# Output projection, feed-forward output and final step on two column tiles, two stores, and row sums ahead of a group's last PV

## The chip, the cores and the metric

The kernel runs on one core of a Trainium2 chip. The metric is the device time of one execution in microseconds (us): 202.74, the median of three runs from 202.69 to 202.88.

## The reference

Eight sequences have one new token each. A decode step of attention over the last 1024 positions of a key and value cache and a small feed-forward block both start from the same row of 448 numbers, and a sigmoid gate mixes their results. Cut to what matters:

```python
x = A_x                                               # 8 x 1 x 448
g = sigmoid((x * gate_w).sum(-1, keepdims=True))
q = x @ wq                                            # 16 heads of 256
k, v = k_cache[:, :, -1024:], v_cache[:, :, -1024:]   # 8 kv heads, each for 2 query heads
p = softmax((q . k) * 256 ** -0.5)
a = concat_heads(p . v) @ wo                          # 4096 -> 448
h = gelu(layernorm(x) @ w1 + b1)                      # 448 -> 1792
b = h @ w2 + b2                                       # 1792 -> 448
return g * a + (1 - g) * b                            # 8 x 1 x 448
```

## The kernel before

All inputs and the output are bf16; sums are kept in float32 in PSUM. A *pair* is one sequence with one kv head: 64 pairs, numbered so that eight in a row share a kv head and make a *group* of eight pairs. Each pair has a K tile and a V tile of 512 KB, and each group has 448 KB of `wo` (`wo_sb[g]`). The kernel reads 78 MB in all.

**Order of the loads.** Lines 121 to 135 issue the small inputs, `w1`, `w2` and `wq` on SP's and ACT's queues. Lines 137 to 164 then lay out one list for SP's queue: K tiles, V tiles eleven pairs behind them, the `wo` part of a group behind its last K tile, and at the very end the last V tiles and `wo_sb[7]`. The K and V tiles share 23 buffers; `issue_to` (line 148) issues the first 23 at once and then one for each tile that has been used.

**Front.** `transposed` (207), `mlp_up` (231) and `mlp_down` (258) do the feed-forward block. `mlp_down` adds 14 matmuls and one for the bias into `b_ps` (lines 261 and 268): the stationary operand is `hT`, with 8 columns for the 8 sequences, and 448 columns of `w2` stream past it. Line 272 scales the result by 1 - g into `bvec`. Lines 280 to 299 make the queries.

**Main loop** (432 to 455), written out by hand, each engine working in program order. Step n transposes the K tile of pair n on TensorE (line 314) and copies it from PSUM on VectorE (319), computes the scores of pair n-1 (330), and does the PV product of pair m = n-11 (396). Once for each group come the maximum (`soft_max1`, `soft_max2`), the exponential (`soft_exp`), and, behind the PV of its last pair, `soft_sum` (380: eight matmuls that add up the rows of the exponentials, line 382, and a reciprocal, 387), `o_scale` (405: the scaling of the PV results into `ot`, line 407). One step later `o_proj` (415) multiplies the group's `ot` by its part of `wo`: four matmuls (421), 8 columns stationary, 448 streamed, all added into `A_ps`. Scores, row sums and PV results of a group lie in one PSUM tile, `grp`.

**End.** Behind the loop stand the last `o_proj` (456), the final step on VectorE, res = A_ps * g + bvec (458), and one store on SP's queue (461).

Of the kernel before, what the change touches and what calls it, by code (L numbers as in the profile page):

```python
# [9 lines left out]
ALU = mybir.AluOpType  # L10
AXIS = mybir.AxisListType
BF16 = mybir.dt.bfloat16
F32 = mybir.dt.float32
# [3 lines left out]
def kernel(  # L17
# [15 lines left out]
    nc = tc.nc  # L33
    P = nc.NUM_PARTITIONS

    B, Sq, D = A_x.shape
    _, Hkv, Sk, Dh = A_k_cache.shape
    HD = A_wq.shape[1]
    Hq = HD // Dh
    rep = Hq // Hkv  # L40
# [3 lines left out]
    NB = B  # L44
    NJ = Dh // P
    NC = W // P
    NF = F // P
# [10 lines left out]
    NKV = 23  # L58


    S0 = 0
    O0 = S0 + NC * R
    Z0 = O0 + NJ * R
# [3 lines left out]
    out_f = out.rearrange("b s d -> (b s) d")  # L67

    consts = ctx.enter_context(tc.tile_pool(name="consts", bufs=1))
# [9 lines left out]
    ps_a = ctx.enter_context(  # L79
        tc.tile_pool(name="ps_a", bufs=1, space=bass.MemoryType.PSUM)  # L80
    )
# [10 lines left out]
    w2_sb = consts.tile([P, NF, D], BF16, name="w2_sb")  # L92
    b2_sb = consts.tile([1, D], BF16, name="b2_sb")
    NKH = rep * NJ
    wo_sb = [consts.tile([P, NKH, D], BF16, name=f"wo_sb{g}") for g in range(Hkv)]
    ident = consts.tile([P, P], BF16, name="ident")
    identf = consts.tile([P, P], F32, name="identf")
    onesb = consts.tile([P, P], BF16, name="onesb")
# [2 lines left out]
    xT = consts.tile([P, DC + 2, NB], BF16, name="xT")  # L101
    yT = consts.tile([P, DC + 1, NB], BF16, name="yT")
    x_e = consts.tile([NB, 2, P], BF16, name="x_e")
    g_sb = consts.tile([NB, 1], F32, name="g_sb")
    omg_sb = consts.tile([NB, 1], F32, name="omg_sb")
    bvec = consts.tile([NB, D], F32, name="bvec")
    res = consts.tile([NB, D], BF16, name="res")


    def k_src(src, n):  # L110
# [58 lines left out]
    for t in diag:  # L169
        nc.gpsimd.memset(t[:], 0.0)  # L170
    nc.gpsimd.memset(x_e[:], 0.0)
    nc.gpsimd.tensor_copy(identf[:], ident[:])
    nc.vector.memset(yT[:], 1.0)


# [2 lines left out]
    gth = consts.tile([NB, 1], F32, name="gth")  # L178
# [15 lines left out]
        y_sb[:], x_sb[:], scalar1=mv[:, 0:1], scalar2=rstd[:],  # L194
        op0=ALU.subtract, op1=ALU.mult,
    )
    nc.vector.tensor_scalar(g_sb[:], gth[:], 0.5, 0.5, op0=ALU.mult, op1=ALU.add)
    nc.vector.tensor_scalar(omg_sb[:], g_sb[:], -1.0, 1.0, op0=ALU.mult, op1=ALU.add)

    A_ps = ps_a.tile([NB, D], F32, name="A_ps")  # L200

    for h in range(2):
        nc.vector.tensor_copy(
# [25 lines left out]
    M = {}  # L229
# [27 lines left out]

    def mlp_down():
        b_ps = ps_g.tile([P, 512], F32, tag="grp", name="b_ps")
        for k in range(NF):  # L260
            nc.tensor.matmul(  # L261
                b_ps[0:NB, 0:D],
                lhsT=M["hT"][:, k * NB : (k + 1) * NB],
                rhs=w2_sb[:, k, :],
                start=(k == 0),
                stop=False,
            )
        nc.tensor.matmul(  # L268
            b_ps[0:NB, 0:D], lhsT=onesb[0:1, 0:NB], rhs=b2_sb[:],
            start=False, stop=True,  # L270
        )
        nc.vector.tensor_scalar_mul(bvec[:], b_ps[0:NB, 0:D], omg_sb[:])  # L272

    mlp_up()
    mlp_down()


    q_ps = ps_g.tile([P, 512], F32, tag="grp", name="q_ps")
    NQ = Hq * NJ
    for c in range(DC + 1):  # L280
        for k in range(NQ):
            if c < DC:
                w, xs = wq_sb[:, c, k * P : (k + 1) * P], xT[:, c, :]
            else:
                h, kk = divmod(k, NQ // 2)
                w, xs = wq_t[:, kk * P : (kk + 1) * P], xT[:, DC + h, :]
            nc.tensor.matmul(
                q_ps[:, k * NB : (k + 1) * NB],
                lhsT=w,
                rhs=xs,  # L290
                start=(c == 0 and k == 0),
                stop=(c == DC),
                skip_group_check=True,
# [14 lines left out]
    def transposes(n):  # L308
        K = KV.pop(("K", n))
        kt = ktpool.tile([P, NJ, W], BF16, tag="kt", name="kt")  # L310
        for j in range(NJ):
            ktp = ps_kt.tile([P, W], BF16, tag="ktp", name="ktp")
            for c in range(NC):
                nc.tensor.transpose(  # L314
                    ktp[:, c * P : (c + 1) * P],
                    K[:, c, j * P : (j + 1) * P],
                    ident[:],
                )
            nc.vector.tensor_copy(kt[:, j, :], ktp[:])  # L319
        KT[n] = kt  # L320

    def scores(n):
        g, b = divmod(n, NB)
        kt = KT.pop(n)
        if b == 0:
            G[g] = ps_g.tile([P, 512], F32, tag="grp", name="grp")
        for c in range(NC):
            for j in range(NJ):
                s = S0 + c * R + b * rep
                nc.tensor.matmul(  # L330
                    G[g][:, s : s + rep],
                    lhsT=kt[:, j, c * P : (c + 1) * P],
                    rhs=qT[:, j, g, b, :],
                    start=(b == 0 and c == 0 and j == 0),
                    stop=(j == NJ - 1),
                    skip_group_check=True,
                )

    def soft_max1(g):
        pm = work.tile([P, R], F32, tag="pm", name="pm")  # L340
        nc.vector.reduce_max(
            pm[:],
            G[g][:, S0 : S0 + NC * R].rearrange("p (c r) -> p r c", r=R),
            axis=AXIS.X,
        )
        G["pm", g] = pm
# [22 lines left out]
    def soft_exp(g):  # L369
        nc.tensor.matmul(  # L370
            G[g][:, S0 : S0 + NC * R].rearrange("p (c r) -> p c r", c=NC),
            lhsT=onesb[:],
            rhs=diag[g % 2][:].unsqueeze(1).to_broadcast([P, NC, R]),
            start=False, stop=True, skip_group_check=True,
        )
        e = work.tile([P, NC * R], BF16, tag="e", name="e")
        nc.scalar.activation(e[:], G[g][:, S0 : S0 + NC * R], ACT.Exp)  # L377
        E[g] = e

    def soft_sum(g):  # L380
        for c in range(NC):
            nc.tensor.matmul(  # L382
                G[g][:, Z0 : Z0 + R], lhsT=onesb[:], rhs=E[g][:, c * R : (c + 1) * R],
                start=False, stop=(c == NC - 1), skip_group_check=True,
            )
        rz = work.tile([P, R], F32, tag="rz", name="rz")
        nc.vector.reciprocal(rz[:], G[g][:, Z0 : Z0 + R])  # L387
        RZ[g] = rz

    def pv(m):  # L390
        g, b = divmod(m, NB)
        V = KV.pop(("V", m))
        for j in range(NJ):
            for c in range(NC):
                o = O0 + j * R + b * rep
                nc.tensor.matmul(  # L396
                    G[g][:, o : o + rep],
                    lhsT=V[:, c, j * P : (j + 1) * P],
                    rhs=E[g][:, c * R + b * rep : c * R + (b + 1) * rep],
                    start=False,  # L400
                    stop=(c == NC - 1),
                    skip_group_check=True,
                )

    def o_scale(g):
        ot = work.tile([P, NJ, R], BF16, tag="ot", name="ot")
        nc.vector.tensor_tensor(  # L407
            ot[:],
            G[g][:, O0 : O0 + NJ * R].rearrange("p (j r) -> p j r", j=NJ),
            RZ[g][:].unsqueeze(1).to_broadcast([P, NJ, R]),  # L410
            op=ALU.mult,
        )
        OT[g] = ot

    def o_proj(g):
        ot = OT[g]
        for i in range(rep):
            for j in range(NJ):
                k = i * NJ + j
                w = wo_sb[g][:, k, :]  # L420
                nc.tensor.matmul(  # L421
                    A_ps[:],
                    lhsT=ot[:].rearrange("p j (b i) -> p j i b", i=rep)[:, j, i, :],
                    rhs=w,
                    start=(g == 0 and k == 0),
                    stop=(g == Hkv - 1 and k == NKH - 1),
                )


    LAST = NPAIR + NB + LAG  # L430
# [1 line left out]
    for n in range(LAST):  # L432
        if n < NPAIR:
            transposes(n)
            done += 1
        if 0 <= n - 1 < NPAIR:
            scores(n - 1)
        g, r = divmod(n, NB)
        if g >= 1 and g - 1 < Hkv:
            if r == 0:  # L440
                soft_max1(g - 1)
            if r == 1:
                soft_max2(g - 1)
            if r == 2:
                soft_exp(g - 1)
        m = n - NB - LAG
        if m >= 0:
            pv(m)
            done += 1
            if m % NB == NB - 1:  # L450
                soft_sum(m // NB)
                o_scale(m // NB)
            if m % NB == 0 and m > 0:
                o_proj(m // NB - 1)
        issue_to(NKV + done)
    o_proj(Hkv - 1)

    nc.vector.scalar_tensor_tensor(  # L458
        res[:], in0=A_ps[:], scalar=g_sb[:], in1=bvec[:], op0=ALU.mult, op1=ALU.add
    )  # L460
    nc.sync.dma_start(out_f, res[:])


# [1 line left out]
_INS = ['A_x', 'A_k_cache', 'A_v_cache', 'A_wq', 'A_wo', 'B_x', 'B_w1', 'B_b1', 'B_w2', 'B_b2', 'gate_w']  # L465
_OUTS = [((8, 1, 448), 'bfloat16')]
# [25 lines left out]
```

## Time and profile before

| | us |
|---|---|
| median of three runs | 202.74 |
| the profiled execution | 202.94 |
| its span, first to last instruction | 201.2 |
| PE (matmul) busy | 161.7 |
| PEld (weight load) busy | 146.6 |
| DVE (VectorE) busy | 106.7 |
| ACT (ScalarE) busy | 5.6 |
| SP's load queue, share of 16 DMA engines | 95.9% |
| mean granted TensorE clock | 0.79 |

The profile comes from one execution. `PE` rows are matmuls and `PEld` rows weight loads, which overlap them; `SPq` and `ACTq` are the queues of SyncE and ScalarE that issue DMAs. A row of the timeline has its start, its duration, the engine, the line in the code, the operation, out<-in with the partitions x elements and types, and in brackets how long the engine had been idle and what released it. In a matmul `128*8 128x448`, 128 x 8 is the stationary operand and 448 the number of streamed columns. A row of the chain of waits has start, duration and what. A row of the windows has the stretch, its length, the busy time of PE, PEld, DVE, ACT and POOL with the number of instructions, the granted clock, the DMA share and GB/s.

### The profile page before, as it was taken

The numbers are of one execution on the slowest core, as the hardware profiler recorded it, in microseconds if no ns is written. First come the engines' busy times: TensorE is split into PE (matmuls) and PEld (weight loads), VectorE is DVE, ScalarE is ACT, GpSimd is POOL, SyncE is SP. The second block draws the span as 40 slices with busy tenths as digits, with TensorE's granted clock in tenths as the row PEclk, the third lists the DMA queues.
The fourth block names the chain that finished last, engine by engine and source line by source line (L and its number), as shares of the span: only waits on it lengthen the run. The fifth ranks groups of instructions, "written<-read, shape, count | busy, mean of one in ns | idle before, by whom it ended". The sixth has DMA issues, their size and how long they took to land.

```text
span 201.2 us, 7399 instructions
## 1 busy us (share of the span) xinstructions
PE 161.7 (80%) x3392; PEld 146.6 (73%) x3392; DVE 106.7 (53%) x241; ACT 5.6 (3%) x13; POOL 1.4 (1%) x11
## 2 busy tenths in 40 slices
PE   0268999987899759979898789777999899785753
PEld 0162799977898759879887789677897898785440
DVE  4220189995575526755495448544673658554001
ACT  3200000000000000000000000000000000000000
POOL 2000000000000000000000000000000000000000
PEclk9999979999669856985599757988556969975555
DMA  5999999999999999999999999999999999999930
GB/s 185 343 415 414 415 416 411 414 415 406 414 419 419 404 418 420 416 407 415 420 415 411 411 420 412 416 414 413 415 425 404 412 416 421 415 415 415 371 133 1
DMA packets 23682, 78.15 MB, mean 389 GB/s; under 512 B 2314, under 2 KB 6435, under 8 KB 23012
## 3 DMA queue, kind: packets, MB, share of 16 engines
q1 hardware_dynamic: 23552, 77.45, 95.9%
q8 instruction: 26, 0.43, 0.8%
q10 hardware_dynamic: 100, 0.24, 0.4%
q14 instruction: 4, 0.03, 0.0%
HBM read 77.68 MB, written 0.01 MB: 386 GB/s over the span
## 4 chain that ended last, share of the span: by engine, by line
DMA 91%; PE 6%; DVE 1%; issue 0%; ACTq 0%; SPq 0%; DVEq 0%
DMA kv<-in_A_v_cache_dram 42%; DMA kv<-in_A_k_cache_dram 40%; DMA wq_t<-in_A_wq_dram 6%; DMA w_t<-in_B_w_dram 4%; PE ktp L314 3%; PE A_ps L421 1%; PE grp L396 1%; PE grp L330 1%; DVE res L458 0%; ACTq L122 0%; DVE rz L387 0%; PE grp L382 0%; DVE ot L407 0%; SPq L118 0%; DVEq L387 0%
## 5 line engine op out<-in xcount | busy, mean ns | idle before, releaser
L319 DVE COPY kt<-ktp 128x1024 bf16<-128x1024 bf16 x128 | 84.2, 688 | 56.5 <-PE ktp L314 56.0
L314 PE MATMUL ktp<-ident,kv 128*128 128x128 bf16 x1024 | 86.2, 252 | 12.6 <-DMA kv<-in_A_k_cache_dram 12.6
L314 PEld LDWEIGHTS <-kv 128*128 128x128 bf16 x1024 | 74.5, 115 | 18.0 <-DMA kv<-in_A_k_cache_dram 16.1
L396 PE MATMUL grp<-e,kv 128*128 128x2 bf16 x1024 | 35.9, 165 | 9.1 <-DMA kv<-in_A_v_cache_dram 7.9
L396 PEld LDWEIGHTS <-kv 128*128 128x128 bf16 x1024 | 32.1, 100 | 13.0 <-DMA kv<-in_A_v_cache_dram 10.4
L330 PE MATMUL grp<-qT,kt 128*128 128x2 bf16 x1024 | 36.3, 165 | 0.3 <-DVE kt L319 0.2
L330 PEld LDWEIGHTS <-kt 128*128 128x128 bf16 x1024 | 34.8, 100 | 0.5 <-DVE kt L319 0.3
L421 PE MATMUL A_ps<-wo_sb,ot 128*8 128x448 bf16 x32 | 9.6, 433 | 0.6 <-DVE ot L407 0.6
L387 DVE RECIPROCAL rz<-grp 128x16 f32<-128x16 f32 x8 | 2.0, 254 | 11.6 <-PE grp L382 11.6
L261 PE MATMUL b_ps<-w_sb,hT 128*8 128x448 bf16 x14 | 5.4, 573 | 2.1 <-DVE hT L255 2.1
L377 ACT ACTIVATE e<-grp 128x128 bf16<-128x128 f32 x8 | 2.2, 278 | 167.3 <-PE grp L370 167.3
L261 PEld LDWEIGHTS <-hT 128*8 128x8 bf16 x14 | 1.6, 122 | 5.2 <-issue 2.9
L421 PEld LDWEIGHTS <-ot 128*8 128x8 bf16 x32 | 2.4, 93 | 3.4 <-issue 1.5
L211 PE MATMUL tp<-ident,y_sb 8*128 8x8 bf16 (+1 forms) x4 | 0.4, 181 | 5.5 <-DVE y_sb L193 5.5
L237 PE MATMUL h_ps<-yT,w_t 65*128 65x8 bf16 x14 | 2.8, 201 | 2.4 <-DMA w_t<-in_B_b_dram 2.4
L211 PEld LDWEIGHTS <-y_sb 8*128 8x128 bf16 (+1 forms) x4 | 0.3, 110 | 5.5 <-DVE y_sb L193 5.5
L237 PE MATMUL h_ps<-yT,w_sb 128*128 128x8 bf16 x42 | 3.5, 202 | 0.7 <-DMA w_sb<-in_B_w_dram 0.7
L237 PEld LDWEIGHTS <-w_sb 128*128 128x128 bf16 x42 | 3.4, 159 | 0.8 <-DMA w_sb<-in_B_w_dram 0.8
L237 PEld LDWEIGHTS <-w_t 65*128 65x128 bf16 x14 | 2.2, 158 | 2.4 <-DMA w_t<-in_B_w_dram 2.4
L249 DVE COPY z<-h_ps 128x112 f32<-128x112 f32 x1 | 0.3, 275 | 6.6 <-PE h_ps L237 6.6
L272 DVE TENSOR_SCALAR bvec<-b_ps,omg_sb 8x448 f32<-8x448 f32 x1 | 0.7, 672 | 5.7 <-PE b_ps L268 5.7
L370 PE MATMUL grp<-diag,onesb 128*128 128x128 bf16 x8 | 1.8, 229 | 2.3 <-DVE diag L364 2.0
(61 smaller groups left out, 44.6 us busy)
## 6 DMA issues: line engine op xcount, KB each, us to landing
kv<-in_A_k_cache_dram SPq DMA_DIRECT2D x64, 512.0 KB, 9.9
kv<-in_A_v_cache_dram SPq DMA_DIRECT2D x64, 512.0 KB, 9.9
wo_sb<-in_A_wo_dram SPq DMA_DIRECT2D x8, 448.0 KB, 9.9
wq_sb<-in_A_wq_dram SPq DMA_DIRECT2D x3, 1024.0 KB, 12.7
w_sb<-in_B_w_dram SPq DMA_DIRECT2D x1, 1568.0 KB, 10.7
w_sb<-in_B_w_dram SPq DMA_DIRECT2D x1, 1344.0 KB
wq_t<-in_A_wq_dram SPq DMA_DIRECT2D x1, 512.0 KB, 11.1
w_t<-in_B_w_dram ACTq DMA_DIRECT2D x1, 224.0 KB, 8.5
```

The lines of the kernel that those rows point to most:

```text
L211: nc.tensor.transpose(tp[0:w, c * NB : (c + 1) * NB], s, ident[0:NB, 0:NB])
L237: nc.tensor.matmul(o, lhsT=w.rearrange("p (q k) -> p k q", k=NF)[:, k, :], rhs=yT[0:kp, c, :], start=(c == 0), stop=(c == DC),)
L261: nc.tensor.matmul(b_ps[0:NB, 0:D], lhsT=M["hT"][:, k * NB : (k + 1) * NB], rhs=w2_sb[:, k, :], start=(k == 0), stop=False,)
L272: nc.vector.tensor_scalar_mul(bvec[:], b_ps[0:NB, 0:D], omg_sb[:])
L314: nc.tensor.transpose(ktp[:, c * P : (c + 1) * P], K[:, c, j * P : (j + 1) * P], ident[:],)
L319: nc.vector.tensor_copy(kt[:, j, :], ktp[:])
L330: nc.tensor.matmul(G[g][:, s : s + rep], lhsT=kt[:, j, c * P : (c + 1) * P], rhs=qT[:, j, g, b, :], start=(b == 0 and c == 0 and j == 0), ...
L370: nc.tensor.matmul(G[g][:, S0 : S0 + NC * R].rearrange("p (c r) -> p c r", c=NC), lhsT=onesb[:], rhs=diag[g % 2][:].unsqueeze(1).to_broadc ...
L377: nc.scalar.activation(e[:], G[g][:, S0 : S0 + NC * R], ACT.Exp)
L387: nc.vector.reciprocal(rz[:], G[g][:, Z0 : Z0 + R])
L396: nc.tensor.matmul(G[g][:, o : o + rep], lhsT=V[:, c, j * P : (j + 1) * P], rhs=E[g][:, c * R + b * rep : c * R + (b + 1) * rep], start=False,
L421: nc.tensor.matmul(A_ps[:], lhsT=ot[:].rearrange("p j (b i) -> p j i b", i=rep)[:, j, i, :], rhs=w, start=(g == 0 and k == 0), stop=(g == ...
```

## The change

The output row of 448 columns is cut into two halves of 224 (`CT`, `DN`). In `o_proj` and `mlp_down` every matmul becomes two, one for each half; the first writes partitions 0 to 7, the second partitions 32 to 39 of a PSUM tile of 64 x 224, and each gets a position in TensorE's array (column 0 or 32). `A_ps`, `bvec` and `res` become 64 x 224. Both PSUM tiles are set to zero first, on VectorE. g and 1 - g are put side by side in `gg`; a small matmul with the matrix `sel` copies them to partitions 32 to 39 as well, as `gg4`. The final step works on 64 partitions and 224 columns, and two stores, on SP's and on ACT's queue, each write one half of the row. In the main loop `soft_sum` is called ahead of the PV of a group's last pair instead of behind it.

```diff
+    CT = 2
+    CP = 32
+    PT = CP * CT
+    DN = D // CT
...
-    bvec = consts.tile([NB, D], F32, name="bvec")
-    res = consts.tile([NB, D], BF16, name="res")
+    gg = consts.tile([NB, 2], F32, name="gg")
+    gg4 = consts.tile([PT, 2], F32, name="gg4")
+    bvec = consts.tile([PT, DN], F32, name="bvec")
+    res = consts.tile([PT, DN], BF16, name="res")
...
+    sel = consts.tile([NB, PT], F32, name="sel")
+    nc.gpsimd.tensor_copy(
+        sel[:].rearrange("b (j q) -> b j q", j=CT),
+        ident[0:NB, 0:CP].unsqueeze(1).to_broadcast([NB, CT, CP]),
+    )
...
-    A_ps = ps_a.tile([NB, D], F32, name="A_ps")
+    A_ps = ps_a.tile([PT, DN], F32, name="A_ps")
+    nc.vector.memset(A_ps[:], 0.0)
...
     def mlp_down():
         b_ps = ps_g.tile([P, 512], F32, tag="grp", name="b_ps")
+        nc.vector.memset(b_ps[0:PT, 0:DN], 0.0)
+        for k in range(NF + 1):
+            for j in range(CT):
+                d = slice(j * DN, (j + 1) * DN)
+                nc.tensor.matmul(
+                    b_ps[CP * j : CP * j + NB, 0:DN],
+                    lhsT=M["hT"][:, k * NB : (k + 1) * NB] if k < NF else onesb[0:1, 0:NB],
+                    rhs=w2_sb[:, k, d] if k < NF else b2_sb[:, d],
+                    start=(k == 0),
+                    stop=(k == NF),
+                    tile_position=(0, CP * j),
+                    skip_group_check=True,
+                )
         nc.tensor.matmul(
+            b_ps[0:PT, DN : DN + 2],
+            lhsT=sel[:],
+            rhs=gg[:], start=False, stop=True, skip_group_check=True,
+        )
+        nc.vector.tensor_copy(gg4[:], b_ps[0:PT, DN : DN + 2])
+        nc.vector.tensor_scalar_mul(bvec[:], b_ps[0:PT, 0:DN], gg4[:, 1:2])
...
     def o_proj(g):
...
+            for h in range(NJ):
+                k = i * NJ + h
+                for j in range(CT):
+                    nc.tensor.matmul(
+                        A_ps[CP * j : CP * j + NB, :],
+                        lhsT=ot[:].rearrange("p j (b i) -> p j i b", i=rep)[:, h, i, :],
+                        rhs=wo_sb[g][:, k, j * DN : (j + 1) * DN],
+                        start=(g == 0 and k == 0),
+                        stop=(g == Hkv - 1 and k == NKH - 1),
+                        tile_position=(0, CP * j),
+                        skip_group_check=True,
+                    )
...
         if m >= 0:
+            if m % NB == NB - 1:
+                soft_sum(m // NB)
             pv(m)
             done += 1
             if m % NB == NB - 1:
-                soft_sum(m // NB)
                 o_scale(m // NB)
...
     nc.vector.scalar_tensor_tensor(
+        res[:], in0=A_ps[:], scalar=gg4[:, 0:1], in1=bvec[:], op0=ALU.mult, op1=ALU.add
+    )
+    for j, eng in enumerate((nc.sync, nc.scalar)):
+        eng.dma_start(
+            out_f[:, j * DN : (j + 1) * DN], res[CP * j : CP * j + NB, :]
+        )
```

More of the change, by code (lines that the diff above doesn't have):

```diff
@@ L58 @@
     NKV = 23
+    CT = 2
+    CP = 32
+    PT = CP * CT
+    DN = D // CT
+    assert D % CT == 0 and NB <= CP
     S0 = 0
@@ L103 @@
     x_e = consts.tile([NB, 2, P], BF16, name="x_e")
-    g_sb = consts.tile([NB, 1], F32, name="g_sb")
-    omg_sb = consts.tile([NB, 1], F32, name="omg_sb")
-    bvec = consts.tile([NB, D], F32, name="bvec")
-    res = consts.tile([NB, D], BF16, name="res")
+    gg = consts.tile([NB, 2], F32, name="gg")
+    gg4 = consts.tile([PT, 2], F32, name="gg4")
+    bvec = consts.tile([PT, DN], F32, name="bvec")
+    res = consts.tile([PT, DN], BF16, name="res")
     def k_src(src, n):
@@ L196 @@
     )
-    nc.vector.tensor_scalar(g_sb[:], gth[:], 0.5, 0.5, op0=ALU.mult, op1=ALU.add)
-    nc.vector.tensor_scalar(omg_sb[:], g_sb[:], -1.0, 1.0, op0=ALU.mult, op1=ALU.add)
-    A_ps = ps_a.tile([NB, D], F32, name="A_ps")
+    nc.vector.tensor_scalar(
+        gg[:, 0:1], gth[:], 0.5, 0.5, op0=ALU.mult, op1=ALU.add
+    )
+    nc.vector.tensor_scalar(
+        gg[:, 1:2], gg[:, 0:1], -1.0, 1.0, op0=ALU.mult, op1=ALU.add
+    )
+    A_ps = ps_a.tile([PT, DN], F32, name="A_ps")
+    nc.vector.memset(A_ps[:], 0.0)
     for h in range(2):
@@ L259, in mlp_down @@
         b_ps = ps_g.tile([P, 512], F32, tag="grp", name="b_ps")
[L260 to L267, printed above, removed]
+        nc.vector.memset(b_ps[0:PT, 0:DN], 0.0)
[11 more added lines that the diff above has]
+                )
         nc.tensor.matmul(
-            b_ps[0:NB, 0:D], lhsT=onesb[0:1, 0:NB], rhs=b2_sb[:],
-            start=False, stop=True,
-        )
-        nc.vector.tensor_scalar_mul(bvec[:], b_ps[0:NB, 0:D], omg_sb[:])
+            b_ps[0:PT, DN : DN + 2],
+            lhsT=sel[:],
+            rhs=gg[:], start=False, stop=True, skip_group_check=True,
+        )
+        nc.vector.tensor_copy(gg4[:], b_ps[0:PT, DN : DN + 2])
+        nc.vector.tensor_scalar_mul(bvec[:], b_ps[0:PT, 0:DN], gg4[:, 1:2])
     mlp_up()
@@ L417, in o_proj @@
         for i in range(rep):
[L418 to L427, printed above, removed]
+            for h in range(NJ):
[10 more added lines that the diff above has]
+                    )
     LAST = NPAIR + NB + LAG
@@ L458 @@
     nc.vector.scalar_tensor_tensor(
-        res[:], in0=A_ps[:], scalar=g_sb[:], in1=bvec[:], op0=ALU.mult, op1=ALU.add
+        res[:], in0=A_ps[:], scalar=gg4[:, 0:1], in1=bvec[:], op0=ALU.mult, op1=ALU.add
     )
-    nc.sync.dma_start(out_f, res[:])
+    for j, eng in enumerate((nc.sync, nc.scalar)):
+        eng.dma_start(
+            out_f[:, j * DN : (j + 1) * DN], res[CP * j : CP * j + NB, :]
+        )
 _INS = ['A_x', 'A_k_cache', 'A_v_cache', 'A_wq', 'A_wo', 'B_x', 'B_w1', 'B_b1', 'B_w2', 'B_b2', 'gate_w']
```

## The prediction

> **What bounds the kernel now.** I read the page first, then the end of the chain of waits, the timeline of the last 15 us, the issues of the last load, and the shares of the DMA engines there.
>
> ```profile
> DMA 91%; PE 6%; DVE 1%; issue 0%; ACTq 0%; SPq 0%; DVEq 0%
> 183.53 11.35 DMA kv<-in_A_v_cache_dram
> ```
>
> The chain is loads for 91% of the span, and its last link is the V tile of the last pair, landed at 194.88. Until then the engines have spare time: from 40 to 180 us PE is busy 121.5 of 140 us, so 18.5 us are idle, some 2.7 us for each group of eight pairs (a group lasts about 21 us). What is on the path is what comes after 194.88:
>
> ```profile
> 186.28 0.38 SPq L153 DMA_DIRECT2D wo_sb<-in_A_wo_dram  x1
> 193.66 0.58 PE L396 MATMUL grp<-e,kv 128*128 128x2 bf16 x16 [0.65 <-DMA kv<-in_A_v_cache_dram]
> 194.92 0.59 PE L396 MATMUL grp<-e,kv 128*128 128x2 bf16 x16 [0.68 <-DMA kv<-in_A_v_cache_dram]
> 195.37 0.36 PE L382 MATMUL grp<-e,onesb 128*128 128x16 bf16 x8
> 195.84 0.26 DVE L387 RECIPROCAL rz<-grp 128x16 f32<-128x16 f32 x1 [10.10 <-PE grp L382]
> 196.13 0.19 DVE L407 TENSOR_TENSOR ot<-grp,rz 128x32 bf16<-128x32 f32 x1
> 196.38 1.66 PE L421 MATMUL A_ps<-wo_sb,ot 128*8 128x448 bf16 x4 [0.65 <-DVE ot L407]
> 196.71 0.13 PEld L421 LDWEIGHTS <-ot 128*8 128x8 bf16 x1 [0.24 <-issue]
> 198.07 0.67 DVE L458 SCALAR_TENSOR_TENSOR res<-A_ps,g_sb,bvec 8x448 bf16<-8x448 f32 x1 [1.75 <-PE A_ps L421]
> 198.77 0.31 SPq L461 DMA_DIRECT2D out_dram<-res  x1
> ```
>
> Each of these waits for the one before it: PV, row sums, reciprocal, scaling, output projection, final step, store; 2.43 us more pass from the store's issue to the end of the span. One thing does not show as a wait: the last weights `wo_sb[7]`, issued at 186.28 behind the last V tile. The view of line 153 and the DMA shares give its landing:
>
> ```profile
> DMA to landing us min/median/max: 9.8/9.9/9.9
> 195.50:195.60 0.10, 0.10 (x9) 0.10 (x6) 0.00 (x0) 0.00 (x0) 0.00 (x0) 0.50 0.13 45
> 195.60:195.70 0.10, 0.10 (x6) 0.04 (x2) 0.00 (x0) 0.00 (x0) 0.00 (x0) 0.50 0.08 27
> 195.70:195.80 0.10, 0.03 (x2) 0.00 (x0) 0.00 (x0) 0.00 (x0) 0.00 (x0) 0.50 0.01 0
> ```
>
> The last two columns are the DMA share and GB/s. Packets run until 195.7, and 186.28 + 9.8 = 196.08 is the landing. Today it is hidden, since the projection starts at 196.38; its slack is only 0.3 us.
>
> **The change, part by part.** All of it counts only after 194.88, if the front and the middle stay covered.
>
> (1) *Row sums and reciprocal ahead of the last PV.* The sums would follow the PV of pair 62: start 193.66 + 0.45 (the step from 194.92 to 195.37), end 0.36 later at 194.47, reciprocal 0.11 later (the gap from 195.73 to 195.84) from 194.58 to 194.84, just ahead of the V tile. PV ends at 195.51, scaling runs from 195.62 to 195.81, and the projection could start 0.06 later at 195.87 instead of 196.38: 0.51 us. But `wo_sb[7]` lands at 196.08, and PE starts 0.04 after a landing (194.88 to 194.92), so the start is 196.12: a gain of 0.26. Half of the stall goes over to a wait for the weights. Ends: 0 and 0.51. If the PV is made to wait for the reciprocal, as both use the tile `grp`, at most 0.06 is lost, inside the 0.25 by which the weights are later. In the middle groups that wait may hold PE behind two copies of 0.69 us on DVE, and behind the PV stand the transposes of the next pair; at most 1.4 us per group against 2.7 us idle.
>
> (2) *Projection in two column tiles.* Four matmuls of 448 columns become eight of 224, with eight weight loads instead of four. At the clock of 0.50 granted there, starts are 0.37 apart (0.83 ns a column), and the last one lasts 0.58, so 0.21 is the fill. Of 224 columns the stream is 0.186. No row here shows two tiles at once, so both ends: one after another, 8 x 0.186 + 0.21 = 1.70, no gain; both at once, 4 x 0.186 + 0.21 = 0.95, and up to 0.09 for the second tile's load. I take 1.00, a gain of 0.66: the operands of the two tiles share no output partitions, and loads already run beside the matmul ahead (196.71 lies inside the first matmul). The third end is above 1.66: if every load stood open, 8 x (0.09 + 0.186) + 0.21 = 2.42; if every matmul also drained, 8 x (0.09 + 0.186 + 0.21) = 3.89.
>
> [...]
>
> (3) *Final step.* 8x448 takes 672 ns; PSUM rows of 128x112 and 128x128 take 275 (line 249) and 300 (line 299), so 1.17 ns an element whatever the partitions. 64x224 is then 672 - 224 x 1.17 = 410 ns, a gain of 0.26 (0.20 to 0.27).
>
> (4) *Two stores.* Nothing is queued behind the new one on ACT, whose last instruction ends near 185. Its issue there costs more than SP's 0.31: rows of ACT's queue at the start are 0.58 (eight rows) to 0.32 (one row), so 0.01 to 0.27 more; I take 0.2. The sixteen rows have 448 bytes instead of eight of 896; the packets of the old store fill only 199.55 to 199.70, so from -0.08 to, as the upper end, another wait like SP's 1.0 us for the store. I add nothing for it.
>
> [...]
>
> (5) *The front.* `mlp_down` goes from 5.4 us for 14 matmuls plus one to thirty of half width: 2.8 us side by side, 5.8 in turn, at worst 30 x 0.49 = 14.6. Two memsets are bounded by 0.09 (128x32) and 0.67 (8x448) each, the `sel` matmul by line 349's 0.38, the copy of `gg4` by 0.14, the cast on POOL by line 172's 0.28. This delays the K transposes that start at 24.8. The cover is the 23 buffers: the 24th K or V load is issued at 44.91 and needs only that pair 0 is transposed, which is done by 27, so 18 us. I cost it at 0; without the cover each us would be one at the end. The same holds for the seven projections in the middle (0.92 us at full clock, 1.65 at half): at worst 3.89, 2.2 to 3.0 more, against 2.7 us idle. SP keeps its loads in their order, and nothing is moved past them.
>
> **Sum:** -0.26 - 0.66 - 0.26 + 0.20 = -0.98. The span of 201.2 becomes 200.2. The profiled execution took 202.94 (1.74 around its span), the median shown is 202.74; against the latter the forecast is 201.75.
>
> **The rivals.**
> A, the forecast: 201.75, its own range 201.2 (0.51, 0.75 and 0.26 gained, the stores free) to 202.2 (half of the tile gain).
> B: the tiles run in turn. For it: no row shows concurrency, and the same number of columns is streamed. -0.26 - 0.26 + 0.20 + 0.04 = -0.28: 202.45.
> C, slower: loads or drains stand open between the tiles of the last projection, 2.42 to 3.89 us in place of 1.66. +0.76 - 0.32 = +0.44 to +2.23 - 0.32 = +1.91: 203.2 to 204.65. It decides from 0.30 us per tiled matmul (1.66 + 0.32 + 0.41 = 2.39 over eight). For it: twice as many loads, each of new weights; against: the load seen beside its matmul.
> D: the half-row stores land late, up to 1.07 more than I take: 202.8. Against: 7 KB with idle DMA engines.
> E: the row sums do not come off the end, for instance because the reciprocal or PV is held: projection at 196.38 as now, 202.0. The margin of 0.04 us between reciprocal and V tile speaks for it, the 0.25 us until the weights land against.
>
> **How the numbers follow.** A 0.66, B 0.13, C 0.08, D 0.06, E 0.05, and 0.02 for a shift of the load stream. Two tenths of a per cent are 0.41 us, about what a measurement of this kernel can tell from no change. Faster: A, E and 0.03 of B, 0.74. Same: 0.10 of B and 0.05 of D, 0.15. Slower: C, 0.01 of D and the rest, 0.11. The range goes from A's low end, 201.2, over B to 202.6; outside are C, part of D and the rest.
>
> **What would show it.** The last projection starting 0.04 after a wait for the DMA of `wo_sb`, and not after `ot`; two matmuls of 224 columns with starts far under 0.19 apart and about 1.0 us for the eight; a final step near 0.41; the ACT store issued within 0.05 of SP's and ending up to 0.27 later; the last V tile landing within 0.3 us of 194.9. Eight matmuls in 1.7 us or more make A wrong; a projection that starts at 195.9 makes the limit by the weights wrong; a last V tile that lands later makes the cover of the front or middle wrong.

## The result, and the profile after

The changed kernel takes 205.69 us (median of four runs, 205.56 to 205.74) against 202.80 for the kernel before in the same measurement: a ratio of 1.0145, 95% interval 1.0132 to 1.0157. It is slower by 1.4%, where 201.75 and a range of 201.2 to 202.6 had been forecast. The profiled execution has a span of 203.9 us, 2.7 more than before.

The timeline of the last microseconds of the changed kernel, in the columns explained above:

```profile
197.54 0.59 PE L421 MATMUL grp<-e,kv 128*128 128x2 bf16 x16 [0.68 <-DMA kv<-in_A_v_cache_dram]
197.99 0.36 PE L407 MATMUL grp<-e,onesb 128*128 128x16 bf16 x8
198.46 0.26 DVE L412 RECIPROCAL rz<-grp 128x16 f32<-128x16 f32 x1 [9.01 <-PE grp L407]
198.80 0.58 PE L421 MATMUL grp<-e,kv 128*128 128x2 bf16 x16 [0.45 <-DMA kv<-in_A_v_cache_dram]
199.43 0.19 DVE L432 TENSOR_TENSOR ot<-grp,rz 128x32 bf16<-128x32 f32 x1 [0.71 <-PE grp L421]
199.93 0.91 PE L446 MATMUL A_ps<-wo_sb,ot 128*8 128x224 bf16 x8 [0.54 <-DMA wo_sb<-in_A_wo_dram]
200.88 0.44 DVE L486 SCALAR_TENSOR_TENSOR res<-A_ps,gg,bvec 64x224 bf16<-64x224 f32 x1 [1.26 <-PE A_ps L446]
201.35 0.31 SPq L490 DMA_DIRECT2D out_dram<-res  x1
201.36 0.31 ACTq L490 DMA_DIRECT2D out_dram<-res  x1
```

Read from the last PV on, this end is what had been forecast, and somewhat better: row sums and reciprocal are over when the last V tile lands, the projection waits for the DMA of `wo_sb`, its eight matmuls take 0.91 us, the final step 0.44. From the start of that PV to the end of the span it is 5.1 us (198.80 to 203.9), where it was 6.3 (194.92 to 201.2). But the PV itself starts 3.9 us later. The time was lost ahead of the end. The windows of the middle of the run show where; the last columns are the granted clock, the DMA share and GB/s. First the kernel before:

```profile
40.00:180.00 140.00, 121.50 (x2617) 114.05 (x2615) 82.78 (x180) 1.95 (x7) 0.00 (x0) 0.79 1.03 415
```

and the changed kernel, with the load queue's row (packets, MB, share of the 16 engines' span) and the chain by engine from its page:

```profile
40.00:180.00 140.00, 127.06 (x2559) 121.95 (x2559) 81.53 (x171) 1.94 (x7) 0.00 (x0) 0.65 1.03 406
```

```profile
q1 hardware_dynamic: 23552, 77.45, 96.3%
...
DMA 62%; PE 27%; DVE 8%; issue 1%; ACTq 0%; ACT 0%; SPq 0%
```

The same 23552 packets and the same 77.45 MB move; the DMA engines are as full as before (1.03), but at 406 GB/s instead of 415, 2.2% less. So here the engines are not starved: the packets take longer. In the records of the trace the 16512 packets of 4096 bytes (rows of K and V tiles and of `wq_t`) take 159.9 ns on average before and 163.4 after. Spread evenly over the 16 engines that is 1032 packets on each, times 3.5 ns: an estimate of 3.6 of the 3.9 us. Not every packet is slower: before, 99% of them take 159 ns; after, 31% still do, 61% take 161 or more, and the slowest hundredth 171 or more. The chain by engine leads astray here: PE's part rose from 6% to 27%, and PE is busier at a lower clock (127.06 us at 0.65 instead of 121.50 at 0.79), yet PE is not what the loads waited for, as the first experiments show.

### The profile page after: what moved, and what is told of

It is laid out like the page before. It is cut to its first block, busy times and chain, and to the rows that moved or that the text cites. A ratio compares the mean times of both kernels' runs of the same rounds, so it can differ in the third digit from the quotient of the medians.

```text
span 203.9 us, 7512 instructions
## 1 busy us (share of the span) xinstructions
PE 167.4 (82%) x3441; PEld 158.5 (78%) x3441; DVE 107.9 (53%) x244; ACT 5.6 (3%) x13; POOL 1.6 (1%) x12
## 3 DMA queue, kind: packets, MB, share of 16 engines
q1 hardware_dynamic: 23552, 77.45, 96.3%
## 4 chain that ended last, share of the span: by engine, by line
DMA 62%; PE 27%; DVE 8%; issue 1%; ACTq 0%; ACT 0%; SPq 0%
DMA kv<-in_A_k_cache_dram 31%; PE ktp L339 18%; DMA kv<-in_A_v_cache_dram 16%; DMA wq_t<-in_A_wq_dram 6%; DMA wo_sb<-in_A_wo_dram 5%; PE grp L421 4%; DMA w_t<-in_B_w_dram 4%; DVE kt L344 4%; PE grp L355 3%; PE A_ps L446 2%; DVE diag L389 1%; DVE rz L412 1%; DVE mx L383 0%; DVE r L385 0%; DVE hi L384 0%
## 5 line engine op out<-in xcount | busy, mean ns | idle before, releaser
L339 PE MATMUL ktp<-ident,kv 128*128 128x128 bf16 x1024 | 96.5, 270 | 7.3 <-DMA kv<-in_A_k_cache_dram 7.0
L339 PEld LDWEIGHTS <-kv 128*128 128x128 bf16 x1024 | 83.7, 124 | 11.5 <-DMA kv<-in_A_k_cache_dram 8.6
L421 PEld LDWEIGHTS <-kv 128*128 128x128 bf16 x1024 | 32.8, 101 | 14.2 <-DMA kv<-in_A_v_cache_dram 10.2
L355 PE MATMUL grp<-qT,kt 128*128 128x2 bf16 x1024 | 37.3, 166 | 0.8 <-issue 0.5
L355 PEld LDWEIGHTS <-kt 128*128 128x128 bf16 x1024 | 36.4, 103 | 1.1 <-issue 0.6
L446 PE MATMUL A_ps<-wo_sb,ot 128*8 128x224 bf16 x64 | 7.2, 380 | 0.5 <-DMA wo_sb<-in_A_wo_dram 0.5
L281 PE MATMUL b_ps<-w_sb,hT 128*8 128x224 bf16 x28 | 2.8, 388 | 2.4 <-DVE b_ps L277 2.4
L432 DVE TENSOR_TENSOR ot<-grp,rz 128x32 bf16<-128x32 f32 x8 | 1.5, 191 | 5.3 <-PE grp L421 5.3
L446 PEld LDWEIGHTS <-ot 128*8 128x8 bf16 x64 | 2.9, 106 | 1.4 <-DVE ot L432 0.4
L407 PE MATMUL grp<-e,onesb 128*128 128x16 bf16 x64 | 3.1, 177 | 0.0
```

What stands on the lines that cost most here:

```text
L281: nc.tensor.matmul(b_ps[CP * j : CP * j + NB, 0:DN], lhsT=M["hT"][:, k * NB : (k + 1) * NB] if k < NF else onesb[0:1, 0:NB], rhs=w2_sb[:, ...
L339: nc.tensor.transpose(ktp[:, c * P : (c + 1) * P], K[:, c, j * P : (j + 1) * P], ident[:],)
L355: nc.tensor.matmul(G[g][:, s : s + rep], lhsT=kt[:, j, c * P : (c + 1) * P], rhs=qT[:, j, g, b, :], start=(b == 0 and c == 0 and j == 0), ...
L407: nc.tensor.matmul(G[g][:, Z0 : Z0 + R], lhsT=onesb[:], rhs=E[g][:, c * R : (c + 1) * R], start=False, stop=(c == NC - 1), skip_group_chec ...
L421: nc.tensor.matmul(G[g][:, o : o + rep], lhsT=V[:, c, j * P : (j + 1) * P], rhs=E[g][:, c * R + b * rep : c * R + (b + 1) * rep], start=False,
L432: nc.vector.tensor_tensor(ot[:], G[g][:, O0 : O0 + NJ * R].rearrange("p (j r) -> p j r", j=NJ), RZ[g][:].unsqueeze(1).to_broadcast([P, NJ, ...
```

## The experiments

### Where the buffers lie

What could make a load slower that the change does not touch? In each partition `bvec` became 896 bytes smaller and `res` 448, `sel` came in with 256, and `gg` and `gg4` took the places of `g_sb` and `omg_sb`. So what is allocated behind them moved down by 1088 bytes, the K and V buffers among it: from byte 112896, which is 441 x 256, to byte 111808, which is 436 x 256 + 192 (addresses of the program's allocation). Theory P: packets are slower when their destination starts off a grid of 128 or 256 bytes. The rivals: T, the new work on PE frees buffers late; H, something else about the program. Four kernels differ only in unused bytes at the end of `res`.

```diff
 # e1, in the changed kernel
-    res = consts.tile([PT, DN], BF16, name="res")
+    res = consts.tile([PT, DN + 32], BF16, name="res")
 # e2, e3, e4 in the kernel before, with n = 32, 16 and 64
-    res = consts.tile([NB, D], BF16, name="res")
+    res = consts.tile([NB, D + n], BF16, name="res")
```

**e1, the changed kernel moved back onto the grid.**

> The changed kernel with the tile res 64 bytes longer per partition (unused bytes), so that the K and V buffers start at byte 111872 of a partition (437 x 256) instead of 111808 (64 bytes past a multiple of 128); no instruction is added or removed. Theory P (placement: the K and V packets are slower when their destination starts off a grid of 128 or 256 bytes): all 4096-byte packets back at 159 ns, last V tile landed near 194.9, 201.5 to 201.9 us. Rival T (the tiled matmuls and the moved row sums slow PE, buffers come free late): as the changed kernel, 205.6 to 205.8. Rival H (the load stream is slower for something that the program brings along, such as where its instructions lie): 205.6 to 205.8.

**e2, the kernel before moved off it by 64 bytes.**

> The kernel before with res 64 bytes longer per partition, so that the K and V buffers start at byte 112960, 64 past a multiple of 128; nothing else differs. Theory P: loads as in the changed kernel (about 406 instead of 415 GB/s in the middle), last V tile near 198.7, 206.3 to 207.0 us. Rivals T and H: 202.7 to 202.9, as the kernel before.

**e3, by 32 bytes.**

> The kernel before with res 32 bytes longer per partition: K and V buffers at byte 112928, 32 past a multiple of 64. Theory P: at least as slow as with 64 bytes, 206.3 us or more. Rivals T and H: 202.7 to 202.9.

**e4, by 128 bytes.**

> The kernel before with res 128 bytes longer per partition: K and V buffers at byte 113024, a multiple of 128 but not of 256. Theory P with a grid of 128 bytes: 202.7 to 202.9; with a grid of 256 bytes: 204 to 207. Rivals T and H: 202.7 to 202.9.

Measured, against 202.57 for the kernel before: e1 201.80 (ratio 0.9956, 0.9942 to 0.9970), e2 206.72 (1.0204, 1.0189 to 1.0219), e3 206.82 (1.0205, 1.0189 to 1.0220), e4 206.49 (1.0192, 1.0177 to 1.0207). The middle of e1, by the windows:

```profile
40.00:180.00 140.00, 121.45 (x2603) 116.81 (x2603) 82.09 (x174) 1.94 (x7) 0.00 (x0) 0.75 1.03 414
```

and of e2:

```profile
40.00:180.00 140.00, 124.36 (x2535) 115.01 (x2533) 81.29 (x176) 1.94 (x7) 0.00 (x0) 0.72 1.03 406
```

Sixty-four unused bytes bring the changed kernel to 414 GB/s, and the same 64 take the kernel before down to 406; the mean packet of 4096 bytes is 159.9 ns in e1 and 163.3, 163.3 and 163.2 in e2 to e4. T and H fall: no instruction differs.

Two more runs ask which grid, and whose address:

```diff
 # g2, in the kernel before: byte 113152, a multiple of 512
+    res = consts.tile([NB, D + 128], BF16, name="res")
 # g4, in the kernel before: 64 bytes between kvpool and ktpool
+    gap = ctx.enter_context(tc.tile_pool(name="gap", bufs=1))
...
+    gap_sb = gap.tile([P, 32], BF16, name="gap_sb")
+    nc.gpsimd.memset(gap_sb[:], 0.0)
```

> The kernel before with res 256 bytes longer per partition: K and V buffers at byte 113152, a multiple of 512 (before: a multiple of 256 only). Theory P with a grid of 256 bytes: as the kernel before, 202.5 to 203.0 us, 415 GB/s. With a grid of 512 bytes on which byte 112896 happened to lie well or badly: another rate, by 1% or more.

> The kernel before with 64 bytes put between the K and V buffers, which stay at byte 112896, and all that lies behind them (the transposed K tiles kt and the work tiles), which move to 64 past a multiple of 128; one small memset on POOL is added. Theory P (only the destination of the loads counts): 202.5 to 203.0 us, 415 GB/s. Rival (what the engines read off the grid slows them and, through them, the loads): 206 to 207 us.

Both are as the kernel before (202.78 there): g2 202.66 (ratio 0.9993, 0.9984 to 1.0003), g4 202.84 (1.0000, 0.9991 to 1.0009). The middle of g4:

```profile
40.00:180.00 140.00, 129.16 (x2600) 120.45 (x2598) 83.36 (x179) 1.95 (x7) 0.00 (x0) 0.68 1.03 414
```

So multiples of 256 are enough (byte 113152 in g2 and byte 112896 in the kernel before both give 415 GB/s), and moving only the transposed tiles and the work tiles, which the engines read, costs nothing (414 GB/s in g4). What counts in these runs is where the loads write. The run g4 also settles what a busier PE at a lower clock is worth: PE is busy for 129.16 us at 0.68, more than the 127.06 of the changed kernel, and the loads keep their 414 GB/s. Over all fourteen profiled executions, the last PV starts between 194.4 and 195.2 us in the ten with the buffers on the grid, and between 198.5 and 198.8 in the four off it.

### The parts of the change, with the buffers on the grid

**f1, the row sums alone.** The kernel before with `soft_sum` ahead of the PV, as in the change.

```diff
+            if m % NB == NB - 1:
+                soft_sum(m // NB)
             pv(m)
             done += 1
             if m % NB == NB - 1:
-                soft_sum(m // NB)
                 o_scale(m // NB)
```

> The kernel before with the row sums and the reciprocal ahead of a group's last PV and nothing else of the change; buffers where they were (byte 112896, a multiple of 256). Theory W (the last weights wo_sb of the last group take over as the bound): the last projection starts 0.26 to 0.32 us earlier, seen against the V tile's landing, released by the DMA of wo_sb; 0.3 us under the kernel before. Rival (full gain): starts 0.5 us earlier, released by ot; 0.5 under. Rival M (the wait of PV for the reciprocal in the middle groups slows the load stream): equal to the kernel before or slower, the last V tile later than 194.9.

Measured 202.57 against 202.84, ratio 0.9986 (0.9976 to 0.9995). The timeline of its end, where the last PV's matmuls start with their first weight load at 194.81:

```profile
194.32 0.26 DVE L387 RECIPROCAL rz<-grp 128x16 f32<-128x16 f32 x1 [9.28 <-PE grp L382]
194.81 0.50 PEld L396 LDWEIGHTS <-kv 128*128 128x128 bf16 x16 [0.69 <-DMA kv<-in_A_v_cache_dram]
...
195.43 0.19 DVE L407 TENSOR_TENSOR ot<-grp,rz 128x32 bf16<-128x32 f32 x1 [0.86 <-PE grp L396]
195.94 1.65 PE L421 MATMUL A_ps<-wo_sb,ot 128*8 128x448 bf16 x4 [0.54 <-DMA wo_sb<-in_A_wo_dram]
```

`ot` is done at 195.62, but the projection starts at 195.94, released by `wo_sb`: 1.13 us after the last PV instead of 1.46 (194.92 to 196.38), a gain of 0.33 and not 0.5. Theory W holds. Rival M falls: PV does wait for the reciprocal (4.3 us in seven waits), and the loads do not notice (the last PV starts at 194.81, before at 194.92).

**f2, the tiles without the row sums.** e1 with the lines of f1 the other way round, `soft_sum` back behind the PV.

> The changed kernel with its buffers at byte 111872 (as the first placement run) and the row sums back behind the PV. The projection then starts after ot, some 1.5 us after the last V tile's landing instead of 1.2; 0.25 to 0.3 us over the first placement run. Rival M: no slower than it.

Measured 201.91, ratio 0.9961 (0.9946 to 0.9976) against e1's 0.9956. The times cannot tell 0.3 us apart here. The timeline can. First f2:

```profile
194.42 0.59 PE L421 MATMUL grp<-e,kv 128*128 128x2 bf16 x16 [0.61 <-DMA kv<-in_A_v_cache_dram]
195.87 0.91 PE L446 MATMUL A_ps<-wo_sb,ot 128*8 128x224 bf16 x8 [0.64 <-DVE ot L432]
```

and e1:

```profile
194.86 0.51 PEld L421 LDWEIGHTS <-kv 128*128 128x128 bf16 x16 [0.49 <-DMA kv<-in_A_v_cache_dram]
194.89 0.57 PE L421 MATMUL grp<-e,kv 128*128 128x2 bf16 x16 [0.42 <-DVE rz L412]
196.06 0.91 PE L446 MATMUL A_ps<-wo_sb,ot 128*8 128x224 bf16 x8 [0.61 <-DMA wo_sb<-in_A_wo_dram]
```

The projection starts 1.45 us after the last PV in f2, released by `ot`, and 1.17 after it in e1, released by `wo_sb`.

**f3 and g1, why eight half matmuls take half the time.** f3 is e1 with the loop over the halves outermost; g1 is the kernel before with half-width matmuls and no column tiles.

```diff
 # f3
+        for j in range(CT):
             for i in range(rep):
                 for h in range(NJ):
                     k = i * NJ + h
-                    for j in range(CT):
 # g1
+                for s in range(2):
+                    d = slice(s * D // 2, (s + 1) * D // 2)
                     nc.tensor.matmul(
-                        A_ps[:],
+                        A_ps[:, d],
...
-                        rhs=w,
+                        rhs=w[:, d],
```

> As the first placement run, with the eight matmuls of each projection in another order: the four of the left half, then the four of the right half. Same instructions, same columns. Theory S (the two column tiles work at the same time when their matmuls alternate): eight matmuls in 1.4 to 1.7 us instead of 0.91, 0.5 to 0.75 us over the first placement run. Rival (half the columns are simply faster each): 0.9 us, no difference.

> The kernel before with each projection matmul cut into two of 224 columns, both in the same place of the array (no column tiles; same partitions, two halves of A_ps). Theory S (the gain of the column tiles is that two work at the same time): starts stay 0.19 us apart at the clock of 0.5, the eight take 1.6 to 1.8 us, the kernel as before (202.5 to 203.0 us). Rival (half the columns are faster each, whatever the tile): 0.9 us for the eight, 0.7 us under the kernel before.

f3 takes 201.69 (0.9944, 0.9928 to 0.9961), no slower than e1, against what theory S expected of it; g1 takes 203.06 against 202.78 (1.0024, 1.0008 to 1.0041), just over the 203.0 that theory S allowed. The projection in the timeline of f3:

```profile
196.37 0.92 PE L446 MATMUL A_ps<-wo_sb,ot 128*8 128x224 bf16 x8 [0.62 <-DMA wo_sb<-in_A_wo_dram]
```

and of g1:

```profile
196.41 1.65 PE L423 MATMUL A_ps<-wo_sb,ot 128*8 128x224 bf16 x8 [0.64 <-DVE ot L407]
```

Half the width in one place of the array gains nothing (1.65 us, 1.66 in the kernel before), so the gain is from two tiles at once, and the rival of "faster halves" falls with g1. What f3 disproves is only that the program has to alternate. The windows over PE's instructions of the projection count the matmuls in flight in the first 0.1 us. In f3 (started 196.37):

```profile
196.38:196.40 0.03, 0.03 (x2) 0.50 0.00 0
196.38:196.48 0.10, 0.10 (x2) 0.50 0.00 0
```

in g1 (started 196.41):

```profile
196.42:196.52 0.10, 0.10 (x1) 0.50 0.00 0
```

In f3 the second matmul of the program is again one of the left half; still two run at once, started within 0.03 us of each other (196.37 to 196.40). In g1, where all lie in one place, only one is in flight until 196.52, 0.11 us behind the start. So the second to start in f3 is taken to be of the right tile, whose first matmul is the fifth in the program. That is inferred from these times: the trace does not name a matmul's tile.

**f4, both stores on SP.**

```diff
-    for j, eng in enumerate((nc.sync, nc.scalar)):
+    for j, eng in enumerate((nc.sync, nc.sync)):
```

> As the first placement run, with both stores on SP's queue. The second store is issued 0.31 us after the first, and the span ends 0.15 to 0.35 us later. Rival (the issue is not on the path, the landing of the half rows is): no difference.

Measured 201.73, ratio 0.9950 (0.9935 to 0.9965), so no loss against e1's 0.9956, though the intervals leave room for 0.3 us. The issues in f4 and then in e1:

```profile
197.03 0.66 SPq L490 DMA_DIRECT2D out_dram<-res  x2
```

```profile
197.48 0.31 SPq L490 DMA_DIRECT2D out_dram<-res  x1
197.49 0.31 ACTq L490 DMA_DIRECT2D out_dram<-res  x1
```

From the first issue to the end of the span it is 2.6 us in f4 (197.03 to 199.6) and 2.5 in e1 (197.48 to 200.0). The expected loss of 0.15 to 0.35 is not there: by these two executions the second queue gains about 0.1 us at most.

**g3, the wait for the last weights.** e1 with the last group's `wo_sb` in two tiles with a load each.

```diff
-    wo_sb = [consts.tile([P, NKH, D], BF16, name=f"wo_sb{g}") for g in range(Hkv)]
+    wo_sb = [[consts.tile([P, NKH, D], BF16, name=f"wo_sb{g}")] for g in range(Hkv - 1)]
+    wo_sb.append([consts.tile([P, NKH // 2, D], BF16, name=f"wo_last{s}") for s in range(2)])
```

> As the first placement run (the changed kernel with its buffers at byte 111872), with the last group's weights in two tiles and two loads of 224 KB. If the last weights bound the projection, its first four matmuls start with ot, about 0.9 us after the last V tile's landing instead of 1.2, only the last four wait, and the span ends 0.3 to 0.5 us earlier: 201.2 to 201.5 us. Rival (the second load costs as much as it hides, or the limit is the DMA's end alone): no difference or slower.

Measured 201.14 against 202.78, ratio 0.9920 (0.9907 to 0.9932): the fastest of all. Its timeline:

```profile
194.56 0.58 PE L424 MATMUL grp<-e,kv 128*128 128x2 bf16 x16 [0.43 <-DMA kv<-in_A_v_cache_dram]
195.18 0.19 DVE L435 TENSOR_TENSOR ot<-grp,rz 128x32 bf16<-128x32 f32 x1 [0.69 <-PE grp L424]
195.43 0.91 PE L449 MATMUL A_ps<-wo_last,ot 128*8 128x224 bf16 x8 [0.28 <-DVE ot L435]
```

The projection starts with `ot`, 0.87 us after the last PV (e1: 1.17), and the eight matmuls run through in 0.91: none waits for the second half of the weights. The row sums then bring what f1 could not. From the last PV to the end of the span g3 takes 4.7 us and e1 5.1, so 0.4 of the gain is shown to come from there. The two ratios lie 0.7 us apart; the rest is ahead of the last PV (194.56 against 194.89), within the spread of the executions on the grid.

## Why the prediction was wrong

**The step that failed** is the one that costs all ahead of 194.88 at nothing: "All of it counts only after 194.88, if the front and the middle stay covered", and in part (5) "I cost it at 0". It weighed whether PE could keep up, found 18 us of cover, and left 0.02 for "a shift of the load stream". The cover held: in e1 all the new instructions are there and the loads run at 414 GB/s. So its own sign, "a last V tile that lands later makes the cover of the front or middle wrong", would have led to the wrong cause. What it did not look at is that the change resizes tiles, and that these lie ahead of the buffers into which nearly all the bytes go. Term missed: 3.9 us at the last V tile (194.92 to 198.80 at its PV), against a forecast gain of 0.98. With loads making up 91% of the chain, the first question should have been what the change does to a load, addresses included; the sizes stand in the diff (896 + 448 - 256 = 1088), and 1088 is not a multiple of 256.

**The rest of the sum** holds, by the changed kernel's own end:

| part | forecast | measured |
|---|---|---|
| (1) start of the projection after the last PV | 1.20 (194.92 to 196.12) | 1.13 (198.80 to 199.93) |
| (2) eight matmuls until the final step starts | 1.00 | 0.95 (199.93 to 200.88) |
| (3) final step | 0.41 | 0.44 |
| (4) ACT's issue beside SP's 0.31 | 0.51 | 0.31 |
| last PV to the end of the span | 5.3 (6.28 less 0.98) | 5.1 |

With the buffers on the grid the whole is 201.80 in e1, beside the 201.75 of case A; against the kernel before of the same measurement (202.57) that is a gain of 0.77 between the medians, where 0.98 was forecast. Part (1): half of the gain goes to the wait for `wo_sb`, as f1 shows alone. Part (2): tiles at once, by g1 and f3; rivals B and C did not come: the eight matmuls took 0.91 us, where the prediction's estimate with every weight load open is 2.42. Part (4): the two stores' price was set too high by 0.1 (2.55 us from SP's issue to the end, 2.43 before), and rival D did not come. Rival E neither: the reciprocal ended at 198.72, 0.08 ahead of the PV. But the margin is as thin as it was said to be: in e1 the last PV was released by the reciprocal, 0.03 us after its first weight load.

The grid of 256 bytes rests on e1 to e4 and g2. The size of the loss is the same at 32, 64 and 128 bytes off: 2.1% each in the mean packet (163.3, 163.3 and 163.2 ns in e3, e2 and e4, 159.9 in e1). Why it is the same for all three stays open.

## What to carry to other kernels

In a kernel bound by loads, compare GB/s in a quiet stretch and the time per packet before reading the chain of waits: an equal share of the DMA engines (1.03) with fewer GB/s (406 instead of 415) meant slower packets here (163.4 ns instead of 159.9), not starved engines. A change of a tile's size can move what is allocated behind it, by 1088 bytes here; start the buffers of the big loads at multiples of 256 bytes, which gave 414 or 415 GB/s here, where 405 or 406 came off them. And when a wait is taken off the end, look at what landed just in time behind it: here the projection started 1.45 us after the last PV in f2, 1.17 in e1, where the last weights took half of the gain, and 0.87 in g3, where cutting their load in two gave it back.

## What the runs showed of the hardware that was not expected

- Loads whose rows of 4096 bytes start 32, 64, 128 or 192 bytes off a multiple of 256 in a partition took 163.2 to 163.4 ns a packet on average instead of 159.9 (e3, e2, e4 and the changed kernel; the kernel before and e1), with 405 or 406 GB/s instead of 414 or 415. The mean penalty had one size here, but the packets differ: 25, 29, 43 and 31% of them still took 159 ns (e3, e2, e4 and the changed kernel).
- Not every row off the grid was slower. In `wo_sb`, which was not moved, rows of 896 bytes start in turn at a multiple of 256 and 128 bytes past one, and 4093 of the 4121 packets of 896 bytes take 41 ns in the kernel before. Why these rows are spared is not shown.
- Matmuls of two column tiles overlapped even when the program has four of one tile ahead of four of the other (the eight took 0.92 us in f3, 1.65 in g1 with one tile).
- Two stores in a row on one queue ended within about 0.1 us of two on two queues (f4), and two stores of half rows of 448 bytes ended about 0.1 later behind SP's issue than one of whole rows: 2.5 us in e1, 2.4 before (both to the end of the span).
